# Token tiles that enter the V projection centred, and first loads split over two DMA-issuing engines

## The chip, the core and the metric

The kernel runs on one core of one Trainium2 chip. The metric is the device time of one execution, in microseconds (us). Each set of runs of a changed kernel was made on the same chip and in the same rounds as runs of the kernel before. A profile is one execution taken by the hardware profiler, so every quoted line is from one execution.

## The reference

The program applies two attention blocks and two token-mixing blocks to a sequence of 2048 tokens of width 1024. Only the beginning matters here.

```python
x = A_x
x = x + _A_ref(_layernorm(x), A_wqkv, A_wo)     # dilated local attention; q, k, v = layernorm(x) @ wqkv
x = x + _B_ref(_layernorm(x), B_w1, ...)        # token-mixing MLP
# both once more
```

## The kernel before

The kernel starts with the V projection of the first layer. A token tile has 128 tokens. For each tile k the kernel loads x, takes mean and variance on VectorE (S, A), takes 1/sqrt(variance) as Ln and Exp on ScalarE (R), normalises on VectorE (N), transposes the tile on TensorE into PSUM (tr), copies it to `hT` on ScalarE (C), multiplies it with two blocks of 512 weight columns (V; n is 0 or 1), and evicts the result on ScalarE (E). Each weight block is loaded in two halves along the contraction. From tile 5 on, a DMA does the transposes, well ahead of need (the first is issued at 19.99 us; the median of the eleven lands 3.1 us after issue). Each engine works through its own list in order; in the run best, below, VectorE stood 2.15 us in front of tile 3's data, though tile 2, next in the list, could have been normalised from about 11.56 on.

```python
for _ in range(14):                       # opening dummy matmuls, 128x512
    chain_("PE", lambda: nc.tensor.matmul(wm[:], lhsT=warm[:, 0:P], rhs=warm[:], start=True, stop=True))
chain_("SP", x_load, 0, halves)           # SyncE issues every load
chain_("SP", x_load, 1)
chain_("SP", w_load, 0, 0)
chain_("SP", x_load, 2)
chain_("SP", w_load, 0, 1)
chain_("SP", x_load, 3)
chain_("SP", w_load, 1, 0)
chain_("SP", w_load, 1, 1)
# ... x_load 4 to 15
pe = [(tr, 0), (V_, 0, 0, lo4), (tr, 1), (V_, 0, 0, hi4), (V_, 1, 0, lo4), (tr, 2), (V_, 1, 0, hi4),
      (V_, 2, 0, a8), (V_, 0, 1, a8), (tr, 3), (V_, 1, 1, a8), (V_, 2, 1, a8), (tr, 4)]   # ... then V of tiles 3 to 15
act = [(R_, 0), (C_, 0, 0), (R_, 1), (C_, 0, 1), (C_, 1, 0), (C_, 1, 1), (R_, 2), (E_, 0, 0), (C_, 2, 0), (C_, 2, 1), ...]
dve = [(S_, 0, 0), (S_, 0, 1), (A_, 0), (S_, 1, 0), (N_, 0, halves), (S_, 1, 1), (A_, 1), (N_, 1, whole),
       (S_, 2, 0), (S_, 2, 1), (A_, 2)]   # then for k = 2..: S(k+1, 0), N(k), S(k+1, 1), A(k+1)
```

V's PSUM results take turns in two buffers (`m`), so the third group of V matmuls needs the first eviction to be over.

The softmax here doesn't subtract the row's maximum and nothing guards it: scores larger than these inputs give would overflow.

## Time and profile before

| | us |
|---|---|
| time before the change, median of 3 (range) | 1295.44 (1294.69 to 1296.03) |
| span of the profiled execution | 1293.7 |
| TensorE busy | 1276.5 (99%) |
| first transpose of tile 0 begins | 7.32 |
| first V matmul of tile 3; no gap on TensorE in V after it | 21.54 |
| last V matmul begins | 66.22 |

The first fence has the busy line of the profile page (engine, busy us, share of the span, number of instructions).

```profile
PE 1276.5 (99%) x8286; PEld 593.7 (46%) x8442; DVE 417.3 (32%) x852; ACT 373.2 (29%) x628; POOL 2.4 (0%) x15
```

TensorE is the bound: what the start loses before V runs without gaps is lost for good, and what it saves is saved, as long as nothing later gives it back. The next fence has TensorE's lines of the timeline up to tile 2, with the VectorE lines that release them. The columns are start in us, busy us of the group, engine, source line, operation, output and inputs, shape and number; in brackets, how long the engine was idle before and what released it.

```profile
1.38 6.11 PE L268 MATMUL m<-warm 128*128 128x512 bf16 x14 [1.38 <-DVE warm L207]
...
5.37 0.73 DVE L188 TENSOR_SCALAR x<-x,mv,rs 128x512 bf16<-128x512 bf16 x2
...
7.32 0.61 PE L244 MATMUL s<-ident,x 128*128 128x128 bf16 x8
...
8.61 1.04 PE L255 MATMUL m<-wv,hT 128*128 128x512 bf16 x4 [0.68 <-ACT hT L249]
...
9.62 0.62 PE L244 MATMUL s<-ident,x 128*128 128x128 bf16 x8
...
10.08 1.89 PE L255 MATMUL m<-wv,hT 128*128 128x512 bf16 x8
...
11.82 0.55 DVE L188 TENSOR_SCALAR x<-x,mv,rs 128x1024 bf16<-128x1024 bf16 x1 [0.26 <-ACT rs L175]
...
12.42 0.62 PE L244 MATMUL s<-ident,x 128*128 128x128 bf16 x8 [0.45 <-DVE x L188]
```

Fourteen dummies run until about 7.3, although tile 0 is normalised at 6.10 (5.37 + 0.73). After the transposes, TensorE waits 0.68 us for the first copy to `hT`, and around 12 us for tile 2's normalisation. Between the dummies (line 268) the spacing is 6.11/14, about 0.43 us; V's 128x512 matmuls come every 0.216 us later. The clock of TensorE doubles somewhere in between (at 7.3 in the clock record of this trace).

### The profile page before, as it was taken

Reading aid. Unit: us, or ns where it says so; the run is one execution under the profiler, and the core shown is the slowest. Engines: PE = TensorE matmul, PEld = TensorE weight load, DVE = VectorE, ACT = ScalarE, POOL = GpSimd, SP = SyncE. Lnnn points to the kernel's source line nnn. Section 1 sums busy time; section 2 is a strip of 40 time slices with the busy share of each in tenths; the row PEclk is TensorE's granted clock in tenths of the full one; section 3 lists DMA queues with packets and bytes.
Section 4 is the critical chain, followed back from the end, with each engine's and each line's share of the span. In section 5 each row is a group of like instructions: output and inputs, shape, how many; then the busy total and the mean of one; then the engine's idle time right before and its main releaser. Section 6 shows DMA issues by size and latency. Waiting matters only on the chain.

```text
span 1293.7 us, 19400 instructions
## 1 busy us (share of the span) xinstructions
PE 1276.5 (99%) x8286; PEld 593.7 (46%) x8442; DVE 417.3 (32%) x852; ACT 373.2 (29%) x628; POOL 2.4 (0%) x15
## 2 busy tenths in 40 slices
PE   9999999999999999999999999999999999999999
PEld 4444444444444444444444444444444444444444
DVE  7457767830000022322300667778100000111111
ACT  5456665541111100000023666644311111000000
POOL 0000000000000000000000000000000000000000
PEclk9999999999999999999999999999999999999999
DMA  7411123643222135456510111246422222334331
GB/s 236 82 44 48 51 80 122 204 138 90 65 78 80 57 101 148 124 155 147 130 33 1 46 51 49 80 151 209 125 66 86 78 59 78 105 106 135 118 92 33
DMA packets 201862, 125.54 MB, mean 97 GB/s; under 512 B 39984, under 2 KB 183600, under 8 KB 201776
## 3 DMA queue, kind: packets, MB, share of 16 engines
q1 hardware_dynamic: 201776, 124.30, 33.9%
q8 instruction: 66, 1.08, 0.3%
q14 instruction: 20, 0.16, 0.0%
HBM read 96.48 MB, written 16.78 MB: 88 GB/s over the span
## 4 chain that ended last, share of the span: by engine, by line
PE 98%; issue 1%; DVE 0%; DMA 0%; ACT 0%; SPq 0%
PE m L352 17%; PE s L594 15%; PE s L547 15%; PE m L467 8%; PE acc L547 7%; PE m L547 7%; PE acc L594 7%; PE m L594 7%; PE m L337 4%; PE m L255 4%; PE s L383 2%; PE acc L418 1%; PE acc L422 1%; PE m L268 0%; DMA qB<-qs 0%
## 5 line engine op out<-in xcount | busy, mean ns | idle before, releaser
L594 PEld LDWEIGHTS <-w 128*128 128x128 bf16 x1820 | 177.0, 98 | 210.2
L547 PEld LDWEIGHTS <-w 128*128 128x128 bf16 x1792 | 175.4, 98 | 211.4
L352 PE MATMUL m<-hT,wqk 128*128 128x512 bf16 x963 | 223.3, 379 | 6.2 <-issue 4.6
L547 PE MATMUL s<-h,w 128*128 128x512 bf16 x878 | 201.2, 379 | 0.8
L594 PE MATMUL s<-g,w 128*128 128x512 bf16 (+1 forms) x912 | 201.0, 374 | 0.7
L596 DVE SCALAR_TENSOR_TENSOR xo<-s,b_sb,xs 128x512 bf16<-128x512 f32 (+1 forms) x33 | 24.4, 739 | 532.9 <-PE s L594 527.6
L352 PEld LDWEIGHTS <-wqk 128*128 128x128 bf16 x1024 | 95.3, 98 | 117.9 <-issue 10.7
L398 DVE TENSOR_TENSOR Pm<-pc,band 32x640 bf16<-32x640 bf16 x256 | 123.5, 483 | 66.0 <-ACT pc L386 56.6
L467 PE MATMUL m<-wo,oT 128*128 128x512 bf16 x500 | 110.6, 379 | 0.8 <-issue 0.3
L547 PE MATMUL acc<-h,w 128*128 128x512 bf16 x440 | 103.1, 379 | 0.5
L594 PE MATMUL acc<-g,w 128*128 128x512 bf16 x436 | 99.7, 379 | 0.5
L547 PE MATMUL m<-h,w 128*128 128x512 bf16 x438 | 98.5, 379 | 0.5
L594 PE MATMUL m<-g,w 128*128 128x512 bf16 (+1 forms) x436 | 96.9, 376 | 0.6
L174 ACT ACTIVATE ln<-mv,eps 128x1 f32<-128x1 f32 x64 | 18.9, 295 | 221.1 <-DVE mv L182 184.9
L467 PEld LDWEIGHTS <-oT 128*128 128x128 bf16 x512 | 49.6, 98 | 60.3 <-issue 1.3
L554 ACT ACTIVATE g<-s,b_sb 128x1024 bf16<-128x1024 f32 x28 | 31.2, 1114 | 158.2 <-PE s L547 146.5
L363 DVE COPY qB<-qs 32x512 bf16<-32x512 bf16 x136 | 38.1, 280 | 90.5 <-ACT qs L359 89.2
L255 PE MATMUL m<-wv,hT 128*128 128x512 bf16 x250 | 55.6, 379 | 1.0 <-ACT hT L249 0.7
L337 PE MATMUL m<-wv,hT 128*128 128x512 bf16 x251 | 55.2, 379 | 0.3
L386 ACT ACTIVATE pc<-s,shift 128x640 bf16<-128x640 f32 x64 | 51.2, 800 | 12.2 <-PE s L383 12.1
L359 ACT CAST qs<-m 128x512 bf16<-128x512 f32 x64 | 37.5, 586 | 49.1 <-PE m L352 48.0
L356 ACT CAST kT<-m 128x512 bf16<-128x512 f32 x64 | 37.5, 586 | 46.4 <-PE m L352 46.4
(58 smaller groups left out, 675.1 us busy)
## 6 DMA issues: line engine op xcount, KB each, us to landing
w<-in_B_w_dram SPq DMA_DIRECT2D x56, 512.0 KB, 3.8
w<-in_B_w_dram SPq DMA_DIRECT2D x64, 448.0 KB, 4.5
wqk<-in_A_wqkv_dram SPq DMA_DIRECT2D x16, 512.0 KB, 4.8
xa<-xn SPq DMA_DIRECT2D x32, 256.0 KB, 2.2
xs<-xa SPq DMA_DIRECT2D x32, 256.0 KB, 3.1
wv<-in_A_wqkv_dram SPq DMA_DIRECT2D x8, 512.0 KB, 5.7
wo<-in_A_wo_dram SPq DMA_DIRECT2D x8, 512.0 KB, 6.0
xr<-in_A_x_dram SPq DMA_DIRECT2D x16, 256.0 KB, 3.3
```

What stands on the lines that cost most here:

```text
L255: r = nc.tensor.matmul(pss_[k, n][:], lhsT=hT[:, kt, cols(*order[k])], rhs=wv[n][kt // 4][:, kt % 4, :], start=(kt == 0), stop=(kt == KD - 1))
L337: nc.tensor.matmul(ps[:], lhsT=hT[:, kt, cols(c, i)], rhs=wv[n][kt // 4][:, kt % 4, :], start=(kt == 0), stop=(kt == KD - 1))
L352: mm = nc.tensor.matmul(ps[:], lhsT=wts[part][:, kt, (g % 2) * P:(g % 2 + 1) * P], rhs=hT[:, kt, lo:lo + 512], start=(kt == 0), stop=(kt = ...
L356: nc.scalar.copy(out=kT[u % 2][:, ls], in_=ps[:])
L359: nc.scalar.copy(out=qs[:], in_=ps[:])
L363: nc.vector.tensor_copy(out=qB[u % 2][hp, h, ls], in_=qs[hp, :])
L386: nc.scalar.activation(out=pc[:].rearrange("p (n t) h k -> p n (t h k)", n=2), in_=ss[:, :, 0:2 * HG * GW], func=ACT.Exp, scale=scale, bia ...
L398: mm = nc.vector.tensor_tensor(out=Pm[rp, :, s0:s0 + HB, r * KG:r * KG + GW].rearrange("p h t k -> p t h k"), in0=pc[rp], in1=mk, op=ALU.mult)
L467: mm = nc.tensor.matmul(ps[:], lhsT=oT[g][:, cols(c, i)], rhs=wo[n][g // 4][:, g % 4, :], start=(g == 0), stop=(g == NG - 1))
L547: nc.tensor.matmul(pairs[fl][0][dc], lhsT=wt[c][:, i, fl * P:(fl + 1) * P], rhs=h2[c][i][:, dc * 512:(dc + 1) * 512], start=(k == 0), stop ...
L554: nc.scalar.activation(out=g[fb][:, fl, :].rearrange("p (n d) -> p n d", n=2), in_=t[:], func=ACT.Gelu_apprx_tanh, bias=b1_sb[:, ft:ft + 1])
L594: nc.tensor.matmul(ap, lhsT=w2t[ft // HF][:, ft % HF, c::DIL], rhs=g[ft // GF][:, ft % GF, lo:lo + w], start=(ft == 0), stop=(ft == FT - 1))
```

## The change

The intent is to begin V sooner. A row scale commutes with a matmul from the left, so tiles 0 and 1 need only have their mean subtracted before the transpose; 1/sqrt(variance) is applied when the result is evicted. Ln and Exp leave the path from data to first matmul. Half of tile 0 is centred on ScalarE, half on VectorE. The loads of tiles 0 and 1 and of V's first weight block are cut in halves that SyncE and ScalarE issue at the same time. The dummies go from 14 to 10 at the start and six come in between real work; the orders on TensorE and ScalarE change; tiles 0 and 1 are normalised and transposed by DMA for the query/key projections at the end of the list. The core of the diff, with cuts at "...":

```diff
-    ln_exp_table()                                   # ScalarE's table load was first
+        def M_(k, h):                                # centre on VectorE
+            return nc.vector.tensor_scalar(out=xc[k][:, h], in0=xs[k][:, h], scalar1=mvs[k][:, 0:1], scalar2=None, op0=ALU.subtract)
+        def Ma(k, h):                                # centre on ScalarE; nm0 is the negated mean
+            return nc.scalar.activation(out=xc[k][:, h], in_=xs[k][:, h], func=ACT.Identity, bias=nm0[:])
         def E_(k, n):
+            if k < 2:
+                return nc.scalar.activation(out=dst, in_=src, func=ACT.Identity, scale=rss[k])
-        for _ in range(14):                          # dummies
+        for _ in range(10):
-        chain_("SP", x_load, 0, halves)
-        ...                                          # the eight load lines shown above
+        for q, eng in enumerate((("SP", nc.sync), ("ACT", nc.scalar))):
+            for k in range(2):
+                chain_(eng[0], x_load, k, halves[q], eng[1])
+            for hf in range(2):
+                chain_(eng[0], w_load, 0, hf, quarters[q], eng[1])
+        chain_("ACT", ln_exp_table)
+        for k, n in ((2, 0), (3, 1)):
+            chain_("SP", x_load, k)
+            chain_("SP", w_load, 1, n)
+        pe = [(tr, 0), (W_, 2), (V_, 0, 0, lo4), (W_, 3), (tr, 1), (V_, 0, 0, hi4), (W_, 1), (V_, 1, 0, a8), (V_, 0, 1, lo4), (V_, 1, 1, lo4), (tr, 2),
+              (V_, 0, 1, hi4), (V_, 1, 1, hi4), (V_, 2, 0, a8), (tr, 3), (V_, 2, 1, a8), (tr, 4)]
+        act = [(Ma, 0, halves[1]), (C_, 0, 0), (C_, 0, 1), (R_, 0), (C_, 1, 0), (C_, 1, 1), (R_, 1), (R_, 2), (E_, 0, 0),
+               (E_, 1, 0), (C_, 2, 0), (C_, 2, 1), (E_, 0, 1), (E_, 1, 1), (R_, 3), (R_, 4), (C_, 3, 0), (C_, 3, 1), (E_, 2, 0), ...]
+        dve = [(S_, 0, 0), (S_, 0, 1), (A_, 0), (B_, 0), (M_, 0, halves[0]), (S_, 1, 0), (S_, 1, 1), (A_, 1), (M_, 1, whole[0]), ...]
```

W is a group of dummy matmuls; B negates the mean.

More of the change, by code (lines that the diff above doesn't have):

```diff
@@ L133 @@
                                 pattern=[[-1, GW]], channel_multiplier=1)
+    mv01 = const.tile([P, 2, 2], FP32, name="mv01")
+    rs01 = const.tile([P, 2], FP32, name="rs01")
+    nm0 = const.tile([P, 1], FP32, name="nm0")
     b1_bf = const.tile([P, FT], BF16, name="b1_bf")
@@ L187, in norm_dve @@
     def norm_dve(dst, x, mean, rs):
-        return nc.vector.tensor_scalar(out=dst, in0=x, scalar1=mean, scalar2=rs[:], op0=ALU.subtract, op1=ALU.mult)
+        return nc.vector.tensor_scalar(out=dst, in0=x, scalar1=mean, scalar2=rs, op0=ALU.subtract, op1=ALU.mult)
     def norm_act(dst, x, mean, rs):
@@ L205, in start_up @@
         np_ = 5
+        xc = [x2(f"xc{k}") for k in range(2)]
         warm = x2("warm", [P, 512])
@@ L208, in start_up, with x_tile, x_load, w_load @@
         xs, tps, pss_, mvs, sts, rss = {}, {}, {}, {}, {}, {}
-        def x_load(k, hs=(slice(0, D),)):
-            c, i = order[k]
-            if k % 2 == 0:
-                x_load.t = gop.tile([P, GF, D], BF16, name="x0", tag="go")
-            xs[k] = x_load.t[:, k % 2, :]
-            for h in hs:
-                r = nc.sync.dma_start(out=xs[k][:, h], in_=xin_v[c, i][:, h])
-            return r
-        def w_load(n, hf):
-            return nc.sync.dma_start(out=wv[n][hf][:], in_=wq_v[:, hf * (KD // 2):(hf + 1) * (KD // 2),
-                                                                2 * D + n * 512:2 * D + (n + 1) * 512])
+        def x_tile(k):
+            if k % 2 == 0:
+                x_tile.t = gop.tile([P, GF, D], BF16, name="x0", tag="go")
+            xs[k] = x_tile.t[:, k % 2, :]
+        def x_load(k, h=slice(0, D), eng=nc.sync):
+            c, i = order[k]
+            return eng.dma_start(out=xs[k][:, h], in_=xin_v[c, i][:, h])
+        def w_load(n, hf, ks=slice(0, KD // 2), eng=nc.sync):
+            lo = hf * (KD // 2)
+            return eng.dma_start(out=wv[n][hf][:, ks, :], in_=wq_v[:, lo + ks.start:lo + ks.stop,
+                                                                   2 * D + n * 512:2 * D + (n + 1) * 512])
         def S_(k, cc):
@@ L228, in A_, with B_ @@
         def A_(k):
-            mvs[k] = st("mv", [P, 2])
-            return nc.vector.bn_aggr(out=mvs[k][:], in_=sts[k][:])
+            mvs[k] = mv01[:, k, :] if k < 2 else st("mv", [P, 2])[:]
+            return nc.vector.bn_aggr(out=mvs[k], in_=sts[k][:])
+        def B_(k):
+            return nc.vector.tensor_scalar(out=nm0[:], in0=mvs[k][:, 0:1], scalar1=-1.0, scalar2=None, op0=ALU.mult)
+        def M_(k, h):
+            return nc.vector.tensor_scalar(out=xc[k][:, h], in0=xs[k][:, h], scalar1=mvs[k][:, 0:1], scalar2=None,
+                                           op0=ALU.subtract)
+        def Ma(k, h):
+            return nc.scalar.activation(out=xc[k][:, h], in_=xs[k][:, h], func=ACT.Identity, bias=nm0[:])
         def R_(k):
-            rss[k] = st("rs", [P, 1])
-            return rsqrt(rss[k][:], mvs[k][:, 1:2], 1.0, eps1)
+            rss[k] = rs01[:, k:k + 1] if k < 2 else st("rs", [P, 1])[:]
+            return rsqrt(rss[k], mvs[k][:, 1:2], 1.0, eps1)
         def N_(k, hs):
@@ L243, in tr @@
             for kt in range(KD):
-                r = nc.tensor.transpose(tps[k][:, kt, :], xs[k][:, kt * P:(kt + 1) * P], ident[:])
+                r = nc.tensor.transpose(tps[k][:, kt, :], (xc[k] if k < 2 else xs[k])[:, kt * P:(kt + 1) * P], ident[:])
             return r
@@ L260, in E_, with W_ @@
             c, i = order[k]
-            return nc.scalar.copy(out=v[c][i][:, n * 512:(n + 1) * 512], in_=pss_[k, n][:])
+            dst, src = v[c][i][:, n * 512:(n + 1) * 512], pss_[k, n][:]
+            if k < 2:
+                return nc.scalar.activation(out=dst, in_=src, func=ACT.Identity, scale=rss[k])
+            return nc.scalar.copy(out=dst, in_=src)
         def T_(k):
             return nc.sync.dma_start_transpose(out=hT[:, :, cols(*order[k])], in_=xs[k])
-        wm = m_tile()
-        for _ in range(14):
-            chain_("PE", lambda: nc.tensor.matmul(wm[:], lhsT=warm[:, 0:P], rhs=warm[:], start=True, stop=True))
+        wm = a_tile()
+        def W_(n):
+            for _ in range(n):
+                r = nc.tensor.matmul(wm[:, 0, :], lhsT=warm[:, 0:P], rhs=warm[:], start=True, stop=True)
+            return r
+        for _ in range(10):
+            chain_("PE", W_, 1)
         halves = (slice(0, D // 2), slice(D // 2, D))
         whole = (slice(0, D),)
-        chain_("SP", x_load, 0, halves)
-        chain_("SP", x_load, 1)
-        chain_("SP", w_load, 0, 0)
-        chain_("SP", x_load, 2)
-        chain_("SP", w_load, 0, 1)
-        chain_("SP", x_load, 3)
-        chain_("SP", w_load, 1, 0)
-        chain_("SP", w_load, 1, 1)
+        quarters = (slice(0, KD // 4), slice(KD // 4, KD // 2))
+        for k in range(NT):
+            x_tile(k)
+        for q, eng in enumerate((("SP", nc.sync), ("ACT", nc.scalar))):
[7 more added lines that the diff above has]
+            chain_("SP", w_load, 1, n)
         for k in range(4, NT):
@@ L284, in start_up @@
         a8 = range(KD)
-        pe = [(tr, 0), (V_, 0, 0, lo4), (tr, 1), (V_, 0, 0, hi4), (V_, 1, 0, lo4), (tr, 2), (V_, 1, 0, hi4),
-              (V_, 2, 0, a8), (V_, 0, 1, a8), (tr, 3), (V_, 1, 1, a8), (V_, 2, 1, a8), (tr, 4)]
+        pe = [(tr, 0), (W_, 2), (V_, 0, 0, lo4), (W_, 3), (tr, 1), (V_, 0, 0, hi4), (W_, 1), (V_, 1, 0, a8), (V_, 0, 1, lo4), (V_, 1, 1, lo4), (tr, 2),
+              (V_, 0, 1, hi4), (V_, 1, 1, hi4), (V_, 2, 0, a8), (tr, 3), (V_, 2, 1, a8), (tr, 4)]
         pe += [(V_, k, n, a8) for k in range(3, NT) for n in range(NDC)]
-        act = [(R_, 0), (C_, 0, 0), (R_, 1), (C_, 0, 1), (C_, 1, 0), (C_, 1, 1), (R_, 2), (E_, 0, 0), (C_, 2, 0), (C_, 2, 1),
-               (E_, 1, 0), (R_, 3), (E_, 2, 0), (R_, 4), (E_, 0, 1), (C_, 3, 0), (C_, 3, 1), (R_, 5), (E_, 1, 1), (R_, 6),
-               (E_, 2, 1), (C_, 4, 0), (C_, 4, 1)]
+        act = [(Ma, 0, halves[1]), (C_, 0, 0), (C_, 0, 1), (R_, 0), (C_, 1, 0), (C_, 1, 1), (R_, 1), (R_, 2), (E_, 0, 0),
+               (E_, 1, 0), (C_, 2, 0), (C_, 2, 1), (E_, 0, 1), (E_, 1, 1), (R_, 3), (R_, 4), (C_, 3, 0), (C_, 3, 1), (E_, 2, 0),
+               (R_, 5), (C_, 4, 0), (C_, 4, 1), (E_, 2, 1), (R_, 6)]
         es = [(E_, k, n) for k in range(3, NT) for n in range(NDC)]
@@ L296, in start_up @@
                 act.append(rs.pop(0))
-        dve = [(S_, 0, 0), (S_, 0, 1), (A_, 0), (S_, 1, 0), (N_, 0, halves), (S_, 1, 1), (A_, 1), (N_, 1, whole),
+        dve = [(S_, 0, 0), (S_, 0, 1), (A_, 0), (B_, 0), (M_, 0, halves[0]), (S_, 1, 0), (S_, 1, 1), (A_, 1), (M_, 1, whole[0]),
                (S_, 2, 0), (S_, 2, 1), (A_, 2)]
@@ L305, in start_up @@
                 dve += [(S_, k + 1, 1), (A_, k + 1)]
+            if k in (8, 9):
+                dve.append((N_, k - 8, whole))
         dve.append((zero_fill,))
         dve.append((cast_biases,))
-        sp = [(T_, k) for k in range(np_, NT)] + [(load_biases,)]
+        sp = [(T_, k) for k in (*range(np_, NT), 0, 1)] + [(load_biases,)]
         qs = {"PE": pe, "ACT": act, "DVE": dve, "SP": sp}
-        need = {cast_biases: lambda: (load_biases,) in done, R_: lambda k: k in mvs, N_: lambda k, h: k in rss, tr: lambda k: (N_, k) in done, C_: lambda k, hf: k in tps,
-                V_: lambda k, n, kts: ((C_, k, 1 if kts[-1] == KD - 1 else 0) in done or (T_, k) in done), E_: lambda k, n: (V_, k, n) in done,
-                T_: lambda k: (N_, k) in done}
+        need = {cast_biases: lambda: (load_biases,) in done, R_: lambda k: k in mvs, N_: lambda k, h: k in rss, tr: lambda k: (N_, k) in done if k > 1 else (M_, k) in done and (k == 1 or (Ma, k) in done),
+                B_: lambda k: k in mvs, M_: lambda k, h: k in mvs, Ma: lambda k, h: (B_, k) in done, C_: lambda k, hf: k in tps,
+                V_: lambda k, n, kts: ((C_, k, 1 if kts[-1] == KD - 1 else 0) in done or (T_, k) in done), E_: lambda k, n: (V_, k, n) in done and k in rss,
+                T_: lambda k: (N_, k) in done and (k > 1 or (E_, k, 1) in done)}
         done = set()
@@ L322, in start_up @@
                     else:
-                        done.add((f, *(args if f is C_ else args[:1])))
+                        done.add((f, *(args if f in (C_, E_) else args[:1])))
     def load_wv():
@@ L603, in gemm2 @@
             mean, rs = stats(xo, 1.0, eps1)
-            norm_dve(xs[:], xo[:], mean, rs)
+            norm_dve(xs[:], xo[:], mean, rs[:])
             nc.sync.dma_start_transpose(out=hT[:, :, cols(c, i)], in_=xs[:])
```

## The prediction

> **What bounds the kernel now.** The busy table gives TensorE 1276.5 of 1293.7 us (99%). The change touches only the start, before the V projection runs without gaps. In the chain of waits, from 21.97 us on, TensorE does 49 V matmuls per 10.74 us (0.219 each) with only 0.05 us breaks until V ends at 66.6 us. So the change is worth what it saves before the first matmul of token tile 3 (21.54 us, timeline). From the first transpose (7.32) to there is 14.2 us, of which 5 x 0.45 + 48 x 0.216 = 12.6 are needed work: 1.6 us of gaps (0.68 before the first V matmuls, waiting for the hT copy; about 0.8 around 12 us, waiting for tile 2's normalisation).
>
> **What changes.**
> 1. Tile 0 no longer waits for Ln, Exp and the 0.73 us normalisation. Statistics end at 4.76 (timeline); a tiny negation (estimate 0.1) and half a tile centred on ScalarE (estimate 0.6, as a 128x512 copy takes 0.57 to 0.59) make it ready at about 5.5, against 6.10. The dummy matmuls go from 14 (until 7.3) to 10 (until about 5.65). The first transpose moves from 7.32 to about 5.7.
> 2. Half of the first loads go to ScalarE: four issues (SyncE's take about 0.45 us each) and the 1.28 us table load, done near 4.1, before it is needed. I expect no gain in bandwidth: x lands 2.4 us after issue in any case[...]; the trace moves 310 to 390 GB/s from 7 us on. W quarters should land in time (estimate 6.5 and 7.5).
> 3. Six dummy matmuls are added between real work (0.22 each warm); most fall into gaps. [...] dummies come every 0.43 us until about 7.0, then transposes run at 0.056. So the earlier real work may still run at half rate for over a microsecond.
> 4. V reordered: ScalarE must now run, in order, copies of tile 1, two rsqrt (0.5 each) and eviction (0.59) before the third PSUM tile is free: near 11.8 to 12.3, a small stall. Rsqrt of tile 3 stands behind eviction (1,1): eviction + rsqrt + normalise = 0.76 + 0.55 + 0.6 = 1.9 us against 1.73 of cover: another 0.2 to 0.3 us before transpose 3, and 0.2 at eviction (2,1).
> 5. Two more normalisations (0.55 each) and DMA transposes (about 2.2 us apart) come behind tile 15, and delay the query/key weights from 48 to about 53 us; needed at 66. Off the critical path.
>
> Tile 3 then starts at 20.6 to 21.2 instead of 21.54. Of the 1.6 us by which the first transpose moves up, about half is given back to the half-rate clock, dummies and ScalarE's queue. Saving 0.3 to 1.4 us, 0.9 likely: 0.07%.
>
> **Prediction:** 1294.5 us, range 1293.2 to 1295.7; faster by over 2%: 0.005, within 2%: 0.99, slower: 0.005.
>
> **Right if:** first transpose at 5.5 to 6.0; V ends 0.3 to 1.4 us before 66.6; nothing after it changes; ScalarE done with its table before 4.8; gaps before transpose 3. **Wrong if:** ScalarE's issues take much longer and hold up the centring (slower); the clock stays at half rate past 9 us[...] (slower by up to 1 us); w lands after 8 us; or the gaps I count vanish, which gives 1.7 us.

The cut passages state what no trace of this case shows. No term of the sum goes with it: of the 1.6 us about half was to be given back, 0.9 to be left, and 1295.4 less 0.9 is 1294.5. Without them, the real work at half rate rests on the dummies' 0.43 us, until about 7.0, in the trace before; that bandwidth would not rise rests on that trace's landings (2.4 and 2.5 us after issue for tile 0's halves) and rates. The 0.1 for the negation, the 6.5 and 7.5 for the weights, and the 0.76 for an eviction are estimates; in the trace before an eviction takes 0.59 us and ends 0.79 us after the start of its group's last matmul.

## The result, and the profile after

The changed kernel took 1296.12 us (median of 6, 1295.46 to 1296.88), against 1295.45 (1294.69 to 1296.03, 6 runs) for the kernel before in the same rounds. The ratio is 1.0006, interval 0.9993 to 1.0019. A ratio is the mean time of one kernel's fast runs over that of the other's fast runs of the same rounds, so it is not quite the ratio of these medians. The predicted gain of about 0.9 us did not come, and the median moved 0.67 us the other way. The 33 runs of the kernel before taken for comparison lie between 1294.57 and 1297.08, with a standard deviation of 0.58 us. A few tenths can therefore only be read from where the work lies in the traces, and, as will be seen, not even from one trace.

The busy line and the timeline of the changed kernel; line 287 is a dummy, 258 a transpose, 269 V.

```profile
PE 1288.9 (100%) x8444; PEld 593.8 (46%) x8444; DVE 417.8 (32%) x854; ACT 373.3 (29%) x629; POOL 2.4 (0%) x15
```

```profile
1.38 4.45 PE L287 MATMUL acc<-warm 128*128 128x512 bf16 x10 [1.38 <-DVE warm L210]
...
5.36 0.72 ACT L244 ACTIVATE xc<-x,nm 128x512 bf16<-128x512 bf16 x1 [1.31 <-DVE nm L237]
...
5.64 1.10 PE L258 MATMUL s<-ident,xc 128*128 128x128 bf16 x8
...
7.42 0.60 PE L269 MATMUL m<-wv,hT 128*128 128x512 bf16 x2
...
8.42 0.59 PE L269 MATMUL m<-wv,hT 128*128 128x512 bf16 x2 [0.40 <-DMA wv<-in_A_wqkv_dram]
...
8.85 0.81 PE L287 MATMUL acc<-warm 128*128 128x512 bf16 x3
...
9.50 0.61 PE L258 MATMUL s<-ident,xc 128*128 128x128 bf16 x8
...
11.02 3.69 PE L269 MATMUL m<-wv,hT 128*128 128x512 bf16 x16
...
11.55 0.28 ACT L176 ACTIVATE ln<-mv,eps 128x1 f32<-128x1 f32 x1
...
11.97 0.67 ACT L277 ACTIVATE v<-m,rs 128x512 bf16<-128x512 f32 x1
...
14.55 0.61 PE L258 MATMUL s<-ident,x 128*128 128x128 bf16 x8
```

The first transpose did come 1.68 us earlier (5.64 against 7.32). At 8.42 stands the first surprise: V's third matmul waited for a DMA, the second half of its first weight block (0.56 us by the start times of the matmuls). Three dummies follow, tile 1's transpose begins at 9.50 (before: 9.62), tile 2's at 14.55 (before: 12.42, but at another place of the order). The busy time of TensorE rose by 12.4 us, but the change adds two matmuls net to the program and this trace has 158 more records: most of the rise is records missing from the trace before, and it says nothing about the time.

The chain of waits of the changed kernel, cut at 67 us (start, us, what), shows it from the other side: the path leads through a weight load.

```profile
1.24 0.46 ACTq L220
...
1.73 6.65 DMA wv<-in_A_wqkv_dram
...
8.42 0.59 PE m L269 x2
9.01 0.65 PE acc L287 x3
...
11.19 3.53 PE m L269 x16
...
16.93 0.69 ACT v L277
...
17.82 0.21 ACT rs L177
...
18.06 0.55 DVE x L190
```

The path leaves ScalarE's queue at 1.7, is with the weights until 8.38, and later (16.9 to 18.6) goes through an eviction, an rsqrt and a normalisation before tile 3's transpose.

What the start times of all matmuls add up to, from the first transpose to tile 3's first V matmul: before 14.2 us, of which 12.6 are work and 1.6 waits; after 15.9 us, with the same 12.6 us of work. The 3.3 us in between are: transposes at the low clock 0.45, the wait for the first copy with two dummies in it 0.88, the wait for weights 0.56, the other four dummies 0.86, and waits at ScalarE's queue 0.5. Tile 3 begins at 21.52 (before 21.54), and two more waits for ScalarE in the next tiles (0.27 and 0.08, neither there before) bring the last V matmul to 66.54, 0.32 us later than before. So in this pair of traces 1.68 us were gained at the front and all given back. The list says where TensorE stood, not why; the experiments do.

The next two fences are the DMA view's issue lines for V's first weights (size, then us from issue to landing), first before, then after.

```profile
wv<-in_A_wqkv_dram SPq DMA_DIRECT2D x1, 512.0 KB, 4.9
```

```profile
wv<-in_A_wqkv_dram SPq DMA_DIRECT2D x1, 256.0 KB, 4.9
wv<-in_A_wqkv_dram ACTq DMA_DIRECT2D x1, 256.0 KB, 6.6
```

Before, the whole half was issued at 2.19 and landed at 7.09. After, its quarters were issued earlier, at 1.72 and 1.73, and landed at 6.61 and 8.38. The data needed first came 1.3 us later. It was not for want of bandwidth: by 9.0 us the load queues of SyncE and ScalarE together had moved 2.23 MB after and 2.06 MB before (summed from the packet records). Nor was the whole quarter late: in the records a load's semaphore counts up in 16 steps as its parts land. Of the late quarter 15 steps had come by 6.70, and the last alone took until 8.38; before, the last two came at 6.69 and 7.09.

### The profile page after: what moved, and what is told of

It is laid out like the page before. It is cut to its first block, busy times and chain, and to the rows that moved or that the text cites. A ratio compares the mean times of both kernels' runs of the same rounds, so it can differ in the third digit from the quotient of the medians.

```text
span 1294.0 us, 19571 instructions
## 1 busy us (share of the span) xinstructions
PE 1288.9 (100%) x8444; PEld 593.8 (46%) x8444; DVE 417.8 (32%) x854; ACT 373.3 (29%) x629; POOL 2.4 (0%) x15
## 4 chain that ended last, share of the span: by engine, by line
PE 98%; DMA 1%; ACT 0%; DVE 0%; ACTq 0%; issue 0%; SPq 0%
PE m L382 17%; PE s L624 15%; PE s L577 15%; PE m L497 9%; PE acc L577 7%; PE acc L624 7%; PE m L577 7%; PE m L624 7%; PE m L367 4%; PE m L269 4%; PE s L413 2%; PE acc L448 1%; PE acc L452 1%; DMA wv<-in_A_wqkv_dram 1%; DMA qB<-qs 0%; ACT hT L263 0%
## 5 line engine op out<-in xcount | busy, mean ns | idle before, releaser
L382 PE MATMUL m<-hT,wqk 128*128 128x512 bf16 x1024 | 231.7, 380 | 0.0
```

Of the source, the lines that this page charges most:

```text
L382: mm = nc.tensor.matmul(ps[:], lhsT=wts[part][:, kt, (g % 2) * P:(g % 2 + 1) * P], rhs=hT[:, kt, lo:lo + 512], start=(kt == 0), stop=(kt = ...
```

## The experiments

My theory A was: the split loads bring the first weights and tile 2 later, and the gain is then lost in a chain through tile 2's data, its rsqrt on ScalarE and the first eviction behind it, in whose shadow the dummies lie. Theory B: the dummies between real work cost what was gained. Theory C: the half-rate clock eats it. "V ends" below means the start of V's last matmul. Every kernel computed a correct result.

### The changed kernel again

> The changed kernel unaltered, for the spread of its trace and of its time. First transpose at 5.6 us, second half of V's first weight block landed at 8.0 to 8.6, V's last matmul at 66.3 to 66.8 (66.54 in the first trace; 66.22 before). Time ratio 1.0000 to 1.0010. If the first trace was an unlucky one, V ends at 66.0 or earlier.

The median was 1295.74 (5 runs, 1295.3 to 1300.4, the last with a mean granted clock of 0.999; before in these rounds 1295.56), ratio 1.0000 (0.9986 to 1.0014). That ratio comes out only without the run of 1300.4 us; with it, the means give 1.0008. The profiled execution was the one of 1300.4 us, and V ended at 68.97, which no theory had expected.

```profile
6.57 0.59 PE L287 MATMUL acc<-warm 128*128 128x512 bf16 x2
...
8.76 1.55 PE L269 MATMUL m<-wv,hT 128*128 128x512 bf16 x4 [1.59 <-DMA wv<-in_A_wqkv_dram]
...
10.10 1.49 PE L287 MATMUL acc<-warm 128*128 128x512 bf16 x3
...
11.38 1.06 PE L258 MATMUL s<-ident,xc 128*128 128x128 bf16 x8
```

This is the timeline. TensorE waited 1.6 us for the first weights (they landed at 8.72; its last dummy had ended at 7.16). Then 128x512 dummies came 0.43 us apart again (10.10 to 11.38 for three) and the eight transposes took 1.06 us instead of 0.61: the clock had fallen back to half. The clock records of this trace have it full from 5.71, half from 9.12 and full again from 12.53 us. It was once in four traces of this kernel.

### Without the dummies, and with one rsqrt moved: two by two

```diff
 # no_fill
-        pe = [(tr, 0), (W_, 2), (V_, 0, 0, lo4), (W_, 3), (tr, 1), (V_, 0, 0, hi4), (W_, 1), (V_, 1, 0, a8), ...
+        pe = [(tr, 0), (V_, 0, 0, lo4), (tr, 1), (V_, 0, 0, hi4), (V_, 1, 0, a8), ...
 # r2_moved
-        act = [..., (R_, 1), (R_, 2), (E_, 0, 0), (E_, 1, 0), ...
+        act = [..., (R_, 1), (E_, 0, 0), (R_, 2), (E_, 1, 0), ...
```

> The changed kernel without the six dummy matmuls between real work. Theory A (the dummies hide in the wait for a PSUM tile, whose eviction stands behind the rsqrt of tile 2, which waits for tile 2's late data): the first V(tile 1) matmuls come 0.8 us earlier but the third PSUM tile is still free only at about 12.65, so V's last matmul moves by 0.0 to 0.2 us. Theory B (the dummies themselves cost what was given back): V ends 0.7 to 0.9 earlier, at about 65.7. Theory C (they keep the clock up): without them the clock doubles later than 7.4 us and V ends later.

> The changed kernel with tile 2's rsqrt placed after the first eviction on ScalarE; dummies kept. Theory A: eviction (0,0) ends at about 12.1 instead of 12.64, but with the dummies TensorE is itself not at that point before 12.75, so V's last matmul moves by 0.0 to 0.2 us only. Rival (the ScalarE queue alone is the bound): 0.5 us earlier.

> Both of these at once. Theory A: the two are in series behind each other's shadow, so together they give 0.5 to 0.8 us at the transpose of tile 2 (13.8 to 14.0 instead of 14.55), more than the sum of the two alone; of this at least 0.3 should be left at V's last matmul. If V ends within 0.2 us of the changed kernel, the loss sits later, in the ScalarE order at tiles 3 and 4.

V ended at 65.92, 66.46 and 65.16, that is 0.62, 0.08 and 1.38 us before the 66.54 of the changed kernel. The two edits together gave twice the sum of the two alone, which has the direction of theory A. But each number is from one trace, and the traces of the unaltered changed kernel (below) spread from 66.15 to 67.16 even without the fall-back. Only the 65.16 of both edits stands well clear of them; the 0.08 is not shown at all, and the factor of two is not either. The clock differed as well: it doubled at 7.3 in the changed kernel's first trace and at 5.7 in that of both edits. The size of the first edit was missed (0.0 to 0.2 expected), because in that trace tile 2's data happened to land 0.42 us earlier (9.47 against 9.89), as they vary with this form of loads. The timeline without dummies shows the wait that appears in their place:

```profile
8.91 2.75 PE L269 MATMUL m<-wv,hT 128*128 128x512 bf16 x12
...
11.05 0.29 ACT L176 ACTIVATE ln<-mv,eps 128x1 f32<-128x1 f32 x1 [0.45 <-DVE mv L234]
...
11.49 1.25 ACT L277 ACTIVATE v<-m,rs 128x512 bf16<-128x512 f32 x2
...
12.21 1.89 PE L269 MATMUL m<-wv,hT 128*128 128x512 bf16 x8 [0.55 <-ACT v L277]
```

V's third group (12.21) waited for an eviction on ScalarE (the write of `v`, line 277), and the eviction stood behind tile 2's Ln, which began at 11.05 when tile 2's statistics were there. With both edits that wait is gone; one of 0.19 us before the fourth group is left. This fits B being half right: the four dummies lie mostly in the shadow of that chain, and cost only once it is out of the way. Theory C is not borne out: without the dummies the clock was at its full rate by V's first matmul at 7.59 (spacing 0.22 us), and with both edits it doubled at 5.7. In the time the gains did not show: 1295.40, 1295.47 and 1295.30 against 1295.56, all ratios 0.9998 to 0.9999 with intervals of plus or minus 0.0013.

### The loads

```diff
 # one_queue: the changed kernel with the loads of the kernel before
-        for q, eng in enumerate((("SP", nc.sync), ("ACT", nc.scalar))): ...
+        chain_("SP", x_load, 0, halves[0]); chain_("SP", x_load, 0, halves[1]); chain_("SP", x_load, 1)
+        chain_("SP", w_load, 0, 0); chain_("SP", x_load, 2); chain_("SP", w_load, 0, 1); chain_("SP", x_load, 3)
+        chain_("SP", w_load, 1, 0); chain_("SP", w_load, 1, 1)
 # halves_one_queue: the eight half loads in order of need, all on SyncE
-        for q, eng in enumerate((("SP", nc.sync), ("ACT", nc.scalar))): ...
+        for k in range(2):
+            for q in range(2): chain_("SP", x_load, k, halves[q])
+        for hf in range(2):
+            for q in range(2): chain_("SP", w_load, 0, hf, quarters[q])
```

The third kernel is the reverse: the kernel before with the loads of the change and the table load behind them.

```diff
 # before_two_queues
-    ln_exp_table()
-        chain_("SP", x_load, 0, halves) ...                                   # the eight load lines
+        for q, eng in enumerate((("SP", nc.sync), ("ACT", nc.scalar))): ...   # as in the change, then ln_exp_table
```

> The changed kernel with the loads of the kernel before: SyncE alone, whole weight halves, the same order (tile 2 ahead of the second weight half); centring, dummies and orders kept. Theory A: V's first weight block lands at about 7.1 instead of 8.4, the 0.56 us wait inside the first V group goes, tile 2's data land at 7.7, and V's last matmul comes 0.4 to 0.8 us earlier than in the changed kernel (about 65.9). Rival (loads side by side help, or at least don't hurt): no gain, or a loss because the second half of tile 0 lands 0.2 us later.

> The kernel before with only the loads of the change (halves over two queues, the table load after them). Tile 0's statistics start about 0.4 us later, yet 14 dummies cover that; the first V matmuls come at 8.6 to 8.8 in any case, tile 2's normalisation ends about as before (12.4) because its rsqrt was waiting anyway. Theory A: V's last matmul within -0.1 to +0.6 us of the kernel before (66.2 to 66.8). Rival (two queues bring data sooner): earlier than 66.1.

> The changed kernel with its eight half loads all issued by SyncE, in the order of need (x0, x0, x1, x1, then the quarters of the first weight block, then of the second), everything else as changed. If it is the two queues side by side that make V's first weights land late and unevenly, they land within 7.0 to 7.4 here and V ends 0.3 to 0.7 us before the changed kernel's 66.54. If it is the halving (more, smaller transfers), they land at 7.9 or later and V ends as in the changed kernel.

V ended at 65.88 in one_queue (0.66 earlier than in the changed kernel), at 67.24 in before_two_queues (1.02 later than in the kernel before, more than the 0.6 that I had allowed, and this although the clock doubled early, at about 4.4), and at 66.16 in halves_one_queue (0.38 earlier than the changed kernel's first trace, as expected, but no earlier than its trace after_look3 below, 66.15; the first weights came at 7.45, just outside the expected range and level with the earliest of the two-queue traces). The 65.88 of one_queue is earlier than all four traces of the changed kernel, and the 67.24 of before_two_queues later than all four of the kernel before. In one_queue TensorE waited for the first weights too, but they were complete at 6.98:

```profile
7.02 1.02 PE L269 MATMUL m<-wv,hT 128*128 128x512 bf16 x4 [0.48 <-DMA wv<-in_A_wqkv_dram]
```

The landing times, from the packet and semaphore records of all traces, are the firmest result:

| loads | traces | V's first weights complete | tile 2 landed |
|---|---|---|---|
| whole halves, SyncE alone, order as before | 6 | 6.98 to 7.15 | 7.63 to 8.33 |
| split, SyncE and ScalarE side by side | 8 | 7.45 to 8.72 | 9.47 to 10.61 |
| split, SyncE alone (tile 2 behind both weight halves) | 1 | 7.45 | 9.72 |
| whole halves, SyncE alone, tile 2 behind both weight halves (the three "best" kernels below) | 3 | 6.93 to 7.26 | 9.07 to 9.44 |

Tile 2 comes later mainly because 1.5 MB stand before it instead of 1.0: it does so on one queue as well. The first weights come with a spread of 1.3 us in the eight traces with two queues, and of 0.33 us in the nine in which SyncE alone issues whole halves. The last of the 16 steps came 0.24 to 1.68 us after the one before it in the former, 0.08 to 0.40 in the latter. Whether it is the two queues or the halving is not settled: the one trace of halves_one_queue shows no spread. A third difference went untested: ScalarE's table load began at 2.7 us in all eight two-queue traces and at 0.8 in all others.

In the changed kernel's first trace SyncE's queue had, by 8.0 us, moved all its own 0.79 MB of early loads and 0.30 MB of later ones (0.65 MB by 9.0), while ScalarE's quarter of the first block landed only at 8.38 and its last early load at 9.20. Both queues moved data at once (from 6 to 8 us SyncE's 0.49 MB, ScalarE's 0.26), so loads that nothing waited for yet moved beside those that V waited for; why one part of a load stayed so far behind is not shown.

In before_two_queues the cost shows at tile 2:

```profile
13.44 0.62 PE L244 MATMUL s<-ident,x 128*128 128x128 bf16 x8 [1.58 <-DVE x L187]
```

TensorE had stood idle 1.58 us for VectorE's normalisation of tile 2, which came at 12.42 before. Its time was 1296.68 (ratio 1.0007, 0.9994 to 1.0021) and so the slowest; that of one_queue was 1296.14 (1.0005, 0.9991 to 1.0018) and that of halves_one_queue 1295.91 (1.0006, 0.9993 to 1.0020), although V ended earlier in both than in the changed kernel's first trace. Their later stages were longer; more on that below. So what the loads cost is shown at V's end, by taking them out of the changed kernel and by putting them into the kernel before. The times alone do not show it: all four runs of one_queue (1295.94 to 1296.27) are as slow as the changed kernel.

### Fewer dummies alone

```diff
-        for _ in range(14):     # in the kernel before, nothing else
+        for _ in range(10):
```

> The kernel before with 10 opening dummies instead of 14 and nothing else. Tile 0 is normalised at 6.10 in its trace while dummies run until 7.3, so the first transpose should move to about 6.2 and V's last matmul come 0.5 to 0.8 us earlier (65.4 to 65.7): a large part of what centring was for, without centring. If the half-rate clock eats it: no gain, or a clock that doubles only after 8 us.

V ended at 65.75, 0.47 us before the first trace of the kernel before; the first transpose began at 6.46, just after the normalisation, which stood on VectorE behind tile 1's statistics and these behind tile 1's data until 5.40; the clock doubled at 7.3. The time was 1294.59 (4 runs, 1294.08 to 1295.12) against 1295.78; ratio 0.9993 (0.9979 to 1.0006). I had expected 0.5 to 0.8 us. The clock doubled late in this trace, so the fair neighbours are the two late-clock traces of the kernel before (66.14 and 66.22, below): this one number is worth 0.4 to 0.5 us there.

### The kernel before again: what one trace is worth

> The kernel before against itself: the ratio must be 1 and shows by how much two sets of runs of one program differ (guess: up to 0.0005). V's last matmul at 66.1 to 66.4; the attention stage between the first query matmul and the first output-projection matmul differs between traces of the same program by 0.3 us or more, as it does between the variants so far (140.4 to 141.9 us), although nothing in it was changed.

The ratio was 1.0001 (0.9988 to 1.0013). But V ended at 65.54 in its trace, 0.7 us earlier than in the trace that the prediction was made from, outside what I expected. The timeline of that execution shows why:

```profile
1.38 4.87 PE L268 MATMUL m<-warm 128*128 128x512 bf16 x14 [1.38 <-DVE warm L207]
...
5.68 0.72 DVE L188 TENSOR_SCALAR x<-x,mv,rs 128x512 bf16<-128x512 bf16 x2
...
6.13 0.72 PE L244 MATMUL s<-ident,x 128*128 128x128 bf16 x8
```

The same 14 dummies took 4.87 us instead of 6.11, since the clock doubled at about 4.8 and not at 7.3. The normalisation is then just in front of the transpose. I therefore took two more traces of each kernel.

> The kernel before, another trace. Its first transpose follows the last of 14 dummies: 6.1 to 6.3 us where the clock doubles before 5.5, up to 7.3 where it doubles later; V's last matmul 65.5 to 66.3 accordingly.

> The changed kernel, another trace. First transpose at 5.2 to 5.7; V's last matmul at 66.3 to 66.8 whatever the clock, since V's first weights come complete only at 7.5 to 8.7 (both halves) and tile 2's data after 9.4; later than 68 if the clock falls back to half in a wait for them.

> The kernel before, a third further trace, as before_look2: first transpose and V's last matmul follow the moment at which the clock doubles, between 6.1 and 7.3 us, and between 65.5 and 66.3.

> The changed kernel, a third further trace, as after_look2: V's last matmul at 66.3 to 66.8 whatever the clock, or later than 68 if the clock falls back to half in a wait for the weights.

The times of these four single runs were 1295.72 and 1294.72 before, 1296.36 and 1296.41 after. The clock column is from the clock records of the traces; the spacing of the matmuls agrees.

| trace | clock doubled at about | first transpose | first weights complete | tile 2 landed | V ends |
|---|---|---|---|---|---|
| before, first | 7.3 | 7.32 | 7.09 | 7.75 | 66.22 |
| before_look2 | 7.2 | 7.25 | 7.10 | 7.99 | 66.14 |
| before_look3 | 6.3 | 6.82 | 7.09 | 7.95 | 65.71 |
| before_again | 4.8 | 6.13 | 7.15 | 8.33 | 65.54 |
| after, first | 7.3 | 5.64 | 8.38 | 9.89 | 66.54 |
| after_look3 | 5.4 | 5.78 | 7.57 | 9.61 | 66.15 |
| after_look2 | 4.3 | 5.84 | 8.57 | 10.61 | 67.16 |
| after_again | 5.7; half again 9.1 to 12.5 | 5.84 | 8.72 | 10.27 | 68.97 |

In the kernel before, V's end follows the clock. In the changed kernel it does not (the earliest clock has the second latest end); it follows the landing of the weights and of tile 2. My bounds for the changed kernel (66.3 to 66.8) were too narrow on both sides, because the landing varies by more than I assumed. On the mean of four traces V ends at 65.90 before and 66.62 in the three traces after without the fall-back: 0.7 us later, the size and sign of what the times of the first rounds show (0.67); in the rounds of after_again the medians were 0.18 apart. The first transposes come at 6.88 and 5.78 on the mean of four: 1.1 us earlier, not 1.7.

### Can centring pay?

```diff
 # best, from the changed kernel
+        loads as in the kernel before, in this order: x0, x0, x1, w(0,0), w(0,1), x2, w(1,0), w(1,1), x3
+        pe = [(tr, 0), (W_, 2), (V_, 0, 0, lo4), (tr, 1), (V_, 0, 0, hi4), (V_, 1, 0, a8), (V_, 0, 1, a8), (tr, 2),
+              (V_, 1, 1, a8), (V_, 2, 0, a8), (tr, 3), (V_, 2, 1, a8), (tr, 4)]
+        act = [(Ma, 0, halves[1]), (C_, 0, 0), (C_, 0, 1), (R_, 0), (C_, 1, 0), (C_, 1, 1), (R_, 1), (E_, 0, 0), (R_, 2),
+               (E_, 1, 0), (E_, 0, 1), (C_, 2, 0), (C_, 2, 1), (R_, 3), (E_, 1, 1), (R_, 4), (E_, 2, 0), (C_, 3, 0), (C_, 3, 1),
+               (R_, 5), (E_, 2, 1), (C_, 4, 0), (C_, 4, 1), (R_, 6)]
 # best2, from best: VectorE normalises tile 2 before it starts tile 3's statistics
-        dve = ... (S_, 3, 0), (N_, 2, whole), ...
+        dve = ... (N_, 2, whole), (S_, 3, 0), ...
```

The kernel `best2_uncentred` has the loads and orders of best2, but normalises tiles 0 and 1 as the kernel before does, with ten opening dummies and no others.

> Centred tiles 0 and 1 as in the change, but loads on SyncE alone in the order of need (both halves of V's first weight column block, then tile 2, then the other block, then tile 3), only the two dummies that fill the wait for the first hT copy, V(0,1) whole before tile 2's transpose, and every eviction ahead of work that is not yet due on ScalarE. Theory A: first transpose at 5.7, tile 3's first V matmul at 19.6 to 20.2, V's last matmul at 64.4 to 65.0, time ratio about 0.9985 to 0.9990 to the kernel before. If the bound is elsewhere (clock or bandwidth): V ends later than 65.5.

> As best, but VectorE normalises tile 2 before it starts the statistics of tile 3, which stood in front of it and waited until 13.1 us for tile 3's data. If that in-order wait is the 1.0 us gap before tile 2's transpose in best, the transpose comes at 13.2 to 13.5 instead of 14.34 and V's last matmul at 64.4 to 64.8 instead of 65.55; time ratio to the kernel before 0.998 to 0.999. If the gap only moves elsewhere, V ends after 65.3.

> The same orders and loads as best2 without centring: tiles 0 and 1 are normalised before their transposes as in the kernel before, ten opening dummies, no others. It tells what centring itself is worth once nothing else is in its way. First transpose at 6.4, V's last matmul 0.5 to 0.8 us later than in best2 (65.0 to 65.4). If centring is worth nothing: the same as best2 within 0.15 us.

In best V ended at 65.55, not by 65.0 as expected. I had moved tile 3's data behind the last weights without seeing that VectorE's list has tile 3's statistics in front of tile 2's normalisation. VectorE's timeline in best, then in best2:

```profile
10.79 0.21 DVE L234 BATCH_NORM_AGGREGATE mv<-bn 128x2 f32<-128x12 f32 x1
...
13.14 0.70 DVE L230 BATCH_NORM_STATS2 bn<-x 128x6 f32<-128x512 bf16 x1 [2.15 <-DMA x<-in_A_x_dram]
...
13.75 0.53 DVE L190 TENSOR_SCALAR x<-x,mv,rs 128x1024 bf16<-128x1024 bf16 x1
```

```profile
10.41 0.21 DVE L234 BATCH_NORM_AGGREGATE mv<-bn 128x2 f32<-128x12 f32 x1
...
11.22 0.55 DVE L190 TENSOR_SCALAR x<-x,mv,rs 128x1024 bf16<-128x1024 bf16 x1 [0.60 <-ACT rs L177]
...
12.72 1.29 DVE L230 BATCH_NORM_STATS2 bn<-x 128x6 f32<-128x512 bf16 x2 [0.96 <-DMA x<-in_A_x_dram]
```

In best, VectorE stood 2.15 us in front of tile 3's data, while tile 2 could have been normalised at about 11.6 (its rsqrt ended at 11.56); in best2 it was normalised at 11.22. V ended at 64.12 in best2 (64.4 to 64.8 expected), 2.1 us before the first trace of the kernel before and 1.8 before the mean of its four. Part of the 1.4 us between best and best2 is the clock as well (6.4 against 4.3): V's first matmul began at 7.30 and 6.97. The times: best 1294.62 (5 runs) against 1295.78, ratio 0.9994 (0.9980 to 1.0008); best2 1293.63 (5 runs, 1293.53 to 1294.09) against 1295.10, ratio 0.9989 (0.9975 to 1.0003). That interval still touches 1, but the slowest of the five runs of best2 is faster than the fastest of the 33 of the kernel before, and of its copies (1294.32).

In best2_uncentred V ended at 65.02, 0.9 us later than in best2. The median was 1294.39 with a wide range (1293.81 to 1297.11; ratio 0.9999, 0.9987 to 1.0012). That points to some worth of centring once the loads and lists let it be, but does not show how much. In best2 the clock doubled at 4.3, in the other at 6.5. And in best2_uncentred the data happened to land later: tile 0's second half at 4.28 (3.63 in best2) and tile 1's at 5.55 (4.74), whose statistics stand in front of tile 0's normalisation there.

### What lay outside the start

The rest of the program should be equal in all traces, and nearly is. The two token-mixing stages of layer 1 together took 386.77 us and the second layer's V 55.25 us in each of the 18 traces. Two parts differ. From the second layer's first token-mixing matmul to the last instruction it took 389.70 us in every trace of the kernel before and 389.93 to 389.94 in every one of the changed kernel; 389.95 in before_two_queues, 389.87 to 389.88 in one_queue, best and best2, but 389.94 in halves_one_queue. As the last matmuls are the same, this 0.24 us is at the program's end, and the records of the last 2.5 us show what it is. SyncE ends the program with five waits, one after the other, among them those for the eight semaphores with which the DMAs take turns. In the kernel before, with 448 DMAs, the semaphore of the last store is in the fifth wait; in the changed kernel, with 453, it is in the second, so that three more waits, about 0.065 us each, come after the last landing, which was itself 0.05 us later. It is not the second queue: halves_one_queue, also with 453 DMAs, has SyncE alone. And the attention stages wait now and then for query blocks that a DMA copies (0.3 to 0.5 us each). Attention with the output projection of layer 1 took 197.21 to 198.08 us in the seven traces without centring and 197.35 to 198.81 in the eleven with it. The ranges overlap, the means are 0.3 apart, and whether the change has a part in it stays open. In the traced run of one_queue, whose V ended 0.3 us before the first trace of the kernel before, an attention stage of 198.57 took that back; its other three runs, as slow, were not traced.

## Why the prediction was wrong

Point by point; the fourth is the step on which the sum failed most:

1. *TensorE is the bound, the change is worth what it saves before V runs without gaps.* TensorE was the bound. In the first pair, V's end moved by 0.32 us and the span by 0.34. That the two agree so closely is luck: the attention stages of the two layers together took 0.22 us less, and the program's end 0.24 more.
2. *The first transpose moves from 7.32 to about 5.7.* The place was right (5.64). What I measured it from was not: 7.32 was a late-clock execution, and over four traces of each the gain is 1.1 us. I asked whether the clock would be slow after, and did not ask whether it had been slow in the trace before (until 7.3).
3. *Tile 0 ready at about 5.5.* This failed. The first half was, but the half on ScalarE ended at 6.08 (5.36 + 0.72), where the normalised tile had ended at 6.10: statistics began 0.4 us later (3.60 against 3.20), the negation took 0.15, and ScalarE 0.72 where I had estimated 0.6. The statistics were late because the halves of tile 0 landed 2.8 and 3.2 us after issue, not 2.4. In the first pair the earlier first transpose came mainly from four dummies fewer, since the normalised tile had lain ready from 6.10 while dummies ran until 7.3. In before_ten_dummies, without centring, it came at 6.46, which is 0.86 of the 1.68 us; there VectorE's list and tile 1's data stood in the way, and what centring itself moved is not separated.
4. *W quarters should land in time (estimate 6.5 and 7.5); no gain in bandwidth.* Some bandwidth was gained (364 against 283 GB/s from 5 to 7 us, 380 against 359 from 7 to 9; 2.23 against 2.06 MB by 9.0), and yet this is the step that failed most: the prediction named "w lands after 8 us" as a way to be wrong, and put nothing for it in the sum. I took the bytes in front of a load for its place in time, as if two queues kept one order. The first half was complete at 8.38, which cost TensorE 0.56 us in the first trace, and the second at 9.20; in one execution (after_again) the wait was 1.6 us, and the clock fell back to half at 9.12.
5. *Tile 2's data were not in the sum at all.* They land 2 us later (9.89 against 7.75), hold up VectorE and ScalarE's rsqrt (from 11.55 in the first trace), and with it the eviction that frees the third PSUM buffer (from 11.97).
6. *About half is given back to the half-rate clock, dummies and ScalarE's queue.* The named stalls were there: 0.27 at eviction (2,1), and 0.22 and 0.19 at evictions (2,0) and (0,1), but only 0.03 before transpose 3. The sum was mis-sized: all was given back, and by V's end 0.3 us more in the first pair, 0.7 on the means.
7. *Nothing after it changes.* The query/key weights did come later without harm, but 0.24 us came in at the program's end, by the order of SyncE's last waits.

## What to carry to other kernels

Here the first weights, issued 0.5 us sooner and from two engines, landed 0.2 to 1.8 us later than the same bytes from one engine in whole halves. So check when the last part of a load lands before you count on a sooner issue, and try the loads that are needed first on one queue. Before shortening a chain of work at a kernel's start, look at what the engine's list puts in front of it (dummies, an rsqrt for a later tile, statistics of data that have not landed): here the orders and the number of dummies, by single traces, were worth as much as the new arithmetic. When a change is worth a microsecond, take several traces of the kernel before as well, since with the moment at which the clock doubled its first transpose moved by 1.2 us.

## What the traces show of the clock and of two issuing engines

- With dummies from 1.38 us on, the clock doubled between 4.0 and 7.3 us over 18 traces (during the 7th to the 14th dummy, where dummies were still running). So a fixed number of dummies ended at no fixed time: 14 of them ended between 6.0 and 7.5 us, which moved the first transpose (6.13 to 7.32 in the kernel before) and makes a single trace of this kernel's start a poor base.
- In one trace (after_again) the clock fell back at 9.12, about 2 us after the beginning of a pause of 1.6 us (7.16 to 8.76), and came back at 12.53; in another with about the same pause (after_look2, 1.83 us between matmul starts against 1.97) it did not. The changes in the first lie 3.41 us apart. The stretch that ended in the fall-back, 5.71 to 9.12, was not idle: TensorE was busy for 1.7 us of it. In the first five stretches of 3.41 us after the doubling, no other trace has so little (the next, 1.8 us, is in before_two_queues and had no fall-back; after_look2, whose pause falls across two stretches, has 2.1 and 2.5). What made the clock fall back, and where a limit lies, is not shown.
- The load needed first landed at 7.45 to 8.72 us in the eight traces with two issuers, and at 6.93 to 7.26 in the nine in which one issued whole halves; two issuers and halving are not fully told apart.
